# Three edits to a fused attention and feed-forward kernel: packed keys of later batches transposed by DMA, one first load of p, and k1's transposes between two sums

## The chip, the cores and the metric

The kernel runs on one NeuronCore of a Trainium2 chip. TensorE (PE) multiplies matrices and does transposes against an identity; its weight loads (PEld) overlap its matmuls. VectorE (DVE), ScalarE (ACT) and GpSimd (POOL) compute; SyncE (SP) issues DMAs, as POOL and ACT can. All DMAs of the core run on 16 DMA engines. The metric is the device time of one execution in microseconds (us), lower is better.

## The reference

The inputs are q, k and v of shape (8 batches, 8 heads, 576 rows, 64), p of shape (8, 8, 32, 64), and two weight matrices. Cut to what matters:

```python
def sm_attn(qq, kk, vv):                 # softmax attention, scale 1/8
    ...
p_packed = sm_attn(p, k, v)              # (8, 8, 32, 64): 32 packed keys per head
out = sm_attn(q, p_packed, p_packed)     # (8, 8, 576, 64)
x = out.transpose(0, 2, 1, 3).reshape(4608, 512)
h = x @ w_in                             # 512 -> 2048
result = (h * cos(h)) @ w_out            # 2048 -> 512
```

## The kernel before

All arithmetic on PE is in bf16 with f32 sums. A batch b passes through these steps, which the profile's lines name:

- `load` (L94) brings k, q and v into kbf, qbf and vbf, cast to bf16 on the way; POOL issues it. `pe_T` (L116) transposes k or q on PE, eight blocks to a group, three groups to a batch, and an engine copies each group into kT or qT (L85 on ACT, L87 on DVE). In later batches `xbar` (L102) does this with one DMA transpose, a crossing, issued on SP.
- `dup_p` (L386) casts p to bf16, `pack_p` (L131) transposes it into P2 (the tile P in the profile; DVE copies at L133).
- `s1` (L143, L152): scores of p against k and their exponential, with the row sums. `a1_pe` (L176) or `a1_xbar` (L166) transposes the result into a1T.
- `pp` (L186): the packed keys, 128 rows (four heads of 32) by two halves y of 64 columns, copied from PSUM into pp_sb as the column blocks y0, y1, y0. `pp_T` (L198) transposes the blocks (y0, y1) and (y1, y0) on PE, and DVE or ACT copies them into ppT.
- `s2` (L143, L231): scores of ppT against q and their exponential a2u. `sums2(b, y)` (L239, L241): one matmul pair with a block of ones gives the column sums of half y, and ACT takes their logarithm into lns. `normalise` (L247, L249): ACT's exponential of minus that, then DVE's product a2n.
- `ppw` (L213): PPW, the packed keys times w_in, in four column pieces n.
- `h_mm` (L263, L267, L270; `h_one`, L289 to L295, for batch 0): 16 chunks fc of h from PPW and a2n, the cosine on ACT, and DVE's product gT. `out_gen` (L351, L357): 16 matmuls of gT with w_out to an output chunk, a copy into osb, and the stores, issued on SP.

The order on every engine is written out by hand: each engine runs its instructions in program order. `warm(n)` (L391) puts n dummy matmuls on PE. The start (batch 0, then batch 1) runs from L393 to L488. From then on one batch's h is interleaved with the output matmuls of the batch before: `set_filler` queues the output matmuls of a batch, and `fill(n)` issues n of them. The loop body `slot(s, hooks, keep, heavy, last)` runs the 16 chunks of batch s; after chunk fc it issues its quota of output matmuls and calls the hooks of that step, and `last` is called between the last h matmuls and what follows them. Hook 7 is `tiled(s)`: two pieces of PPW, and `pp` of the next batch. Ahead of each slot s from 3 on stand `fill(5)`, `s2(s)`, `ppw`, `s1(s + 1)`, `a1_xbar(s + 1)`, `xbar("q", s + 1)`, `xbar("k", s + 2)` and `sums2`; POOL waits at `behind(...)` (L98) until the last crossing has landed and then issues the loads of the batches to come.

PSUM: the pool psA has three double banks, the pool O (the tile ot) two single banks; in the start `bank` hands out ot. The tiles pp_sb and ppT have two buffers each, by the parity of the batch.

Of the kernel before, what the change touches and what calls it, by code (L numbers as in the profile page):

```python
# [9 lines left out]
BF16 = mybir.dt.bfloat16  # L10
# [5 lines left out]
def kernel(  # L16
# [10 lines left out]
    nc = tc.nc  # L27
    B, H, S, D = q.shape
# [11 lines left out]
    const = ctx.enter_context(tc.tile_pool(name="const", bufs=1))  # L40
# [22 lines left out]
    V, ACT, G = nc.vector, nc.scalar, nc.gpsimd  # L63
# [3 lines left out]
    ident = const.tile([128, 128], BF16, name="ident")  # L67
# [3 lines left out]
    p_raw = const.tile([128, 2 * B, D], FP32, name="p_raw")  # L71
    p_bf = const.tile([128, 2 * B, 2, D], BF16, name="p_bf")
    a1 = [const.tile([128, 2, C, 128], BF16, name=f"a1_{i}") for i in range(2)]

    pp_sb = [const.tile([128, 3, D], BF16, name=f"pp_sb{i}") for i in range(2)]
    ppT = [const.tile([128, 2, H // 2, NP], BF16, name=f"ppT{i}") for i in range(2)]

    p_rows = p.rearrange("b h n d -> (b h n) d").rearrange("(g r) d -> r g d", r=128)
# [4 lines left out]
    def copy(eng, out, in_):  # L83
        if eng is ACT:
            ACT.copy(out=out, in_=in_)  # L85
        else:
            eng.tensor_copy(out=out, in_=in_)  # L87

    def psa(dt=FP32):
        return psum["A"].tile([128, 2, 512 if dt == FP32 else 1024], dt, name="psA", tag="A")  # L90

    def load(n, b):
        bf[n, b] = bf_pool.tile([TP, H, C * D], BF16, name=n + "bf", tag=n + "bf", bufs=1 if n == "q" else 2)
        G.dma_start(out=bf[n, b], in_=srcs[n][b].rearrange("h (p c) d -> p h (c d)", c=C))  # L94
# [12 lines left out]
    def pe_T(n, b, engs=(V, V, V), groups=(0, 1, 2), own=None):  # L107
        if 0 in groups:
            xT[n, b] = att_pool.tile([128, H * 3, TP], BF16, name=n + "T", tag=n + "T", bufs=2 if n == "k" else 1)
        t = xT[n, b]  # L110
        flat = bf[n, b].rearrange("p h x -> p (h x)")
        for i in groups:
            ps = own(BF16) if own else psa(BF16)[:, 0, :]
            for j in range(8):
                o = 8 * i + j
                nc.tensor.transpose(ps[:, j * TP:(j + 1) * TP], flat[:, o * 128:(o + 1) * 128],  # L116
                                    ident[0:TP, 0:TP])
            to = t[:, 8 * i:8 * i + 8].rearrange("p a x -> p (a x)"), ps[:, 0:8 * TP]
            if engs[i] is None:
                return to  # L120
            copy(engs[i], *to)

    def bank(dt=FP32):
        return O.tile([128, 512 if dt == FP32 else 1024], dt, name="ot", tag="ot")

    def pack_p(b0, b1, flat=None):
        ng = 2 * (b1 - b0)
        if flat is None:
            flat = psa(BF16).rearrange("p a x -> p (a x)")
        for g in range(ng):  # L130
            nc.tensor.transpose(flat[:, g * 128:(g + 1) * 128],  # L131
                                p_bf[:, 2 * b0 + g].rearrange("p t d -> p (t d)"), ident)
        V.tensor_copy(out=P2[:, b0:b1].rearrange("p b h n -> p (b h n)"), in_=flat[:, 0:ng * 128])  # L133
# [45 lines left out]
    def pp(b, eng=V, own=None):  # L179

        ps = own() if own else psa()[:, 0, :]
        for y in range(2):
            for j in range(C):
                c = 2 * (j % 3) + j // 3
                for x in range(4):
                    nc.tensor.matmul(ps[32 * x:32 * x + 32, y * D:(y + 1) * D],  # L186
                                     a1T[b][0:TP, y, j, 32 * x:32 * x + 32],
                                     bf["v", b][:, 2 * x + y, c * D:(c + 1) * D],
                                     start=(j == 0), stop=(j == C - 1))
        t = pp_sb[b % 2].rearrange("p a d -> p (a d)")  # L190
        copy(eng, t[:, 0:2 * D], ps[:, 0:2 * D])
        copy(eng, t[:, 2 * D:3 * D], ps[:, 0:D])

    def pp_T(b, eng=V, own=None):
        ps = own(BF16) if own else psa(BF16)[:, 0, :]
        t = pp_sb[b % 2].rearrange("p a d -> p (a d)")
        for i in range(2):
            nc.tensor.transpose(ps[:, i * 128:(i + 1) * 128], t[:, i * D:i * D + 128], ident)  # L198
        copy(eng, ppT[b % 2].rearrange("p i x n -> p (i x n)"), ps[:, 0:256])

    def ppw(b, n, eng=None, own=False, later=False, cuts=((0, 512),)):
# [25 lines left out]
    def s2(b):  # L227
        a2u[b] = att_pool.tile([128, 2, S], BF16, name="a2u", tag="a2u")
        ps = scores(lambda r, h, e: ppT[b % 2][r, (h + e) % 2, h // 2, :], xT["q", b])
        for y in range(2):  # L230
            ACT.activation(out=a2u[b][:, y].rearrange("p (e x) -> p e x", e=2),  # L231
                           in_=ps[y][:, :, 0:HS], func=AF.Exp, scale=rs1[b][:, y:y + 1])

    def sums2(b, y):
        if b not in lns:
            lns[b] = att_pool.tile([128, 2, S], FP32, name="lns", tag="lns")
        ps = psa()
        for e in range(2):
            nc.tensor.matmul(ps[:, e, 0:HS], ones_blk, a2u[b][:, y, e * HS:(e + 1) * HS],  # L239
                             start=True, stop=True)  # L240
        ACT.activation(out=lns[b][:, y].rearrange("p (e x) -> p e x", e=2),  # L241
                       in_=ps[:, :, 0:HS], func=AF.Ln)
# [141 lines left out]
    def dup_p(a, b, eng):  # L384
        for t in range(2):
            eng.tensor_copy(out=p_bf[:, a:b, t, :], in_=p_raw[:, a:b, :])  # L386

    def warm(n, wps=None, w=None):
        wps, w = bank() if wps is None else wps, wz if w is None else w
        for _ in range(n):  # L390
            nc.tensor.matmul(wps, w[:, 0:128], w, start=True, stop=True)  # L391

    nc.sync.dma_start(out=p_raw[:, 0:2, :], in_=p_rows[:, 0:2, :])  # L393
    load("k", 0)
    load("v", 0)
    make_identity(nc, ident)
    load("q", 0)
    G.dma_start(out=p_raw[:, 2:4, :], in_=p_rows[:, 2:4, :])
    load("k", 1)
    for n in range(3):  # L400
        load_w_in(n)
# [2 lines left out]
    wz4 = const.tile([128, 512], FP32, name="wz4")  # L404
# [6 lines left out]
        V.memset(t[:, :, :, TP:128], 0.0)  # L411

    warm(2, None, wz4)
    dup_p(0, 2, V)
    pack_p(0, 1)
    warm(1, None, wz4)
    warm(3)
    pe_T("k", 0, (V, ACT, V))
    s1(0)
    load_w_in(3)  # L420
    load("v", 1)
    warm(3)
    a1_pe(0)
    warm(2)
    recips(0)
# [1 line left out]
    warm(1)  # L427
    pp_T(0)
    pe_T("q", 0, (V, ACT, V))
    dup_p(2, 4, V)  # L430
    load("q", 1)
    for n in range(4):
        load_w_out(n)
    G.dma_start(out=p_raw[:, 4:, :], in_=p_rows[:, 4:, :])
    load("k", 2)
    s2(0)
    pack_p(1, 2, bank(BF16))
    warm(1)
    sums2(0, 0)
    sums2(0, 1)  # L440
    pe_T("k", 1, (V, V, V), own=bank)
    warm(1)
    normalise(0)
    s1(1)
# [45 lines left out]
    def slot(s, hooks, keep=0, heavy={}, last=None):  # L490


        left = to_do() - keep
        weight = [1 + heavy.get(fc, (0, 0))[0] for fc in range(NFC)]
        for fc in range(NFC):
            rest = h_mm(s, fc)
            if fc == NFC - 1 and last:
                last()
            rest()
            quota = (left * sum(weight[:fc + 1])) // sum(weight) - (left + keep - to_do())  # L500
            behind = min(quota, heavy[fc][1]) if fc in heavy else quota
            fill(quota - behind)
            while hooks and hooks[0][0] == fc:
                hooks.pop(0)[1]()
            fill(behind)
# [5 lines left out]
    def tiled(b):  # L511


        own, later = spare[0], []
        for n in (2, 3):
            later += ppw(b, n, (ACT, V)[n - 2], later=True)
        later[0]()
        pp(b + 1, V, own=lambda: own)
        later[1]()
# [10 lines left out]
    def cross(n, b):  # L530
# [41 lines left out]
                                in_=p_bf[:, 8:2 * B].rearrange("p g t d -> p (g t d)"))  # L572
# [7 lines left out]
    for s in range(3, B):  # L580
        nxt = s + 1 < B
        ACT.preload_act_table_set(EXP_SET)
        osb_eng[0] = V
        set_filler(s - 1)
        fill(5)
        s2(s)
        ppw(s, 0, V)
        fill(8 if nxt else 9)
        if nxt:
            s1(s + 1)  # L590
            ppw(s, 1, V)
            a1_xbar(s + 1)
            xbar("q", s + 1)
            recips(s + 1)
            if s + 2 < B:
                xbar("k", s + 2)
                behind(xT["k", s + 2][0:1, 0, 0:1])
        else:
            for n in range(1, 4):
                ppw(s, n, V)  # L600
        fill(4 if nxt else 5)
        sums2(s, 0)
        fill(5)
        sums2(s, 1)
        normalise(s)
        ACT.preload_act_table_set(SIN_SET)
        fill(13)
        osb_eng[0] = ACT
        for n, b in (("v", s + 2), ("q", s + 2), ("k", s + 3)):
            if b < B:  # L610
                load(n, b)
        if nxt:
            slot(s, [(7, lambda: tiled(s))], 5 if s % 2 else 13, {7: (5, 4)}, lambda: pp_T(s + 1, V))
        else:
            slot(s, [], 5)
    set_filler(B - 1)
# [32 lines left out]
```

## Time and profile before

| | |
|---|---|
| median of 3 runs | 245.64 us (244.95 to 245.83) |
| profiled execution | 245.78 us, its span 244.0 us, granted clock 1.0 |
| PE, DVE, ACT busy | 95%, 67%, 68% of the span |
| PE matmuls of L351, L263 | 485 of 379 ns, 448 of 286 ns (pipelined) |
| loads of k, q, v, median to landing | 13.6, 10.2, 7.8 us |
| crossings of qT, a1T, kT, median to landing | 6.1, 5.5, 4.9 us |

The profile is one execution. Times are counted from the start of its span. A matmul's duration is that of its whole way through the pipeline; matmuls follow each other sooner than that. Lines of the timeline give start, duration, engine, line, operation, output and input, how many instructions are merged, and in brackets the idle time of the engine before them and what ended it. In the DMA views q0 is the queue of POOL's DMAs, q1 that of SP's, and q8 brings instructions.

### The profile page before, as it was taken

To read this page: it belongs to the slowest core of one execution; us is meant where nothing else is said; L and a number is where in the kernel's file an instruction comes from. 1 tells how busy PE (TensorE), PEld (TensorE's weight loads), DVE (VectorE), ACT (ScalarE), POOL (GpSimd) and SP (SyncE) were. 2 spreads that over 40 slices of the span, in tenths; PEclk is the share of its full clock that TensorE was granted. 3 is DMA by queue.
4 is the path that set the end of the run, shared out by engine and by line. 5 is a ranking of instruction groups with operands and counts; after the bars stand their busy time and mean duration, and the time that the engine had idled before them with its cause. 6 is when DMAs were issued, how large, how long until landed. Compare 5 with 4: busy or idle time off the path is not lost.

```text
span 244.0 us, 5461 instructions
## 1 busy us (share of the span) xinstructions
PE 231.8 (95%) x2220; PEld 129.0 (53%) x2255; DVE 162.5 (67%) x259; ACT 166.0 (68%) x267; POOL 38.1 (16%) x61
## 2 busy tenths in 40 slices
PE   7978899999999999999999999999999999999994
PEld 3444254566446564556455654656455645665453
DVE  3349996777568786678758685878657878774001
ACT  2357999778568687877787697858797676774110
POOL 8523230210410032005100410030101010011000
PEclk9999999999999999999999999999999999999999
DMA  6999999999799999997999995999292111311133
GB/s 87 203 211 206 204 206 227 203 233 179 166 171 171 227 176 186 208 224 130 227 224 196 163 219 128 187 165 182 59 192 53 36 46 43 86 32 57 44 85 86
DMA packets 64152, 37.37 MB, mean 153 GB/s; under 512 B 36624, under 2 KB 59536, under 8 KB 64128
## 3 DMA queue, kind: packets, MB, share of 16 engines
q0 software_dynamic: 23184, 18.81, 50.6%
q1 hardware_dynamic: 40704, 18.09, 35.7%
q8 instruction: 17, 0.28, 0.5%
q10 hardware_dynamic: 240, 0.13, 0.2%
q14 instruction: 7, 0.06, 0.1%
HBM read 37.22 MB, written 9.44 MB: 191 GB/s over the span
## 4 chain that ended last, share of the span: by engine, by line
PE 81%; DVE 6%; issue 2%; ACT 1%; ACTq 0%
PE ot L351 48%; PE psA L263 22%; DVE gT L295 3%; PE psA L213 3%; PE psA L143 2%; PE psA L239 2%; PE ot L337 1%; PE psA L186 1%; DVE gT L270 1%; DVE PPW L87 1%; ACT cosT L267 1%; ACT cosT L294 0%; PE psA L116 0%; DVE qT L87 0%; PE psA L303 0%
## 5 line engine op out<-in xcount | busy, mean ns | idle before, releaser
L351 PE MATMUL ot<-w_out_bf,gT 128*128 128x512 bf16 x485 | 128.9, 379 | 2.2 <-issue 1.6
L270 DVE TENSOR_TENSOR gT<-psA,cosT 128x576 bf16<-128x576 f32 x112 | 83.3, 757 | 21.0 <-ACT cosT L267 19.9
L267 ACT ACTIVATE cosT<-psA 128x576 bf16<-128x576 f32 x112 | 72.9, 652 | 24.9 <-PE psA L263 23.5
L263 PE MATMUL psA<-a2n,PPW 128*128 128x288 bf16 x448 | 73.3, 286 | 0.3
L351 PEld LDWEIGHTS <-gT 128*128 128x128 bf16 x512 | 48.2, 98 | 39.5 <-issue 4.2
L263 PEld LDWEIGHTS <-PPW 128*128 128x128 bf16 x448 | 43.8, 98 | 30.1 <-issue 0.4
L87 DVE CAST PPW<-psA 128x1024 bf16<-128x1024 f32 (+1 forms) x24 | 26.8, 1132 | 6.8 <-PE psA L213 6.6
L85 ACT COPY osb<-ot 128x512 f32<-128x512 f32 (+1 forms) x23 | 13.1, 569 | 16.2 <-PE ot L351 13.2
L87 DVE COPY osb<-ot 128x512 f32<-128x512 f32 (+2 forms) x15 | 9.7, 645 | 20.3 <-PE ot L337 17.2
L274 POOL COPY joint<-gT 128x512 bf16<-128x512 bf16 x14 | 8.6, 616 | 83.8 <-DVE gT L270 83.8
L249 DVE SCALAR_TENSOR_TENSOR a2n<-a2u,r,lns 128x576 bf16<-128x576 bf16 x16 | 12.4, 815 | 9.2 <-ACT lns L247 9.2
L152 ACT ACTIVATE a<-psA 128x576 bf16<-128x576 f32 x16 | 10.2, 646 | 9.5 <-PE psA L143 9.5
L241 ACT ACTIVATE lns<-psA 128x576 f32<-128x576 f32 x16 | 10.3, 650 | 7.2 <-PE psA L239 6.7
L351 PE MATMUL ot<-w_out_bf,joint 128*128 128x512 bf16 x45 | 11.7, 380 | 0.2
L231 ACT ACTIVATE a2u<-psA,rs 128x576 bf16<-128x576 f32 x16 | 11.0, 736 | 1.1 <-PE psA L143 1.0
L98 POOL COPY gate<-kT 1x1 bf16<-1x1 bf16 x4 | 0.7, 178 | 68.0 <-DMA kT<-kbf 68.0
L247 ACT ACTIVATE lns<-lns 128x576 f32<-128x576 f32 x16 | 10.0, 673 | 0.0
L213 PE MATMUL psA<-w_in_bf,ppT 64*32 64x512 bf16 x224 | 9.8, 379 | 0.0
L391 PE MATMUL ot<-wz 128*128 128x512 bf16 (+1 forms) x15 | 8.0, 645 | 1.9 <-DVE wz L405 1.7
L295 DVE TENSOR_TENSOR gT<-psH,cosT 128x512 bf16<-128x512 f32 x15 | 9.3, 684 | 0.4 <-ACT cosT L294 0.4
L294 ACT ACTIVATE cosT<-psH 128x512 bf16<-128x512 f32 x15 | 8.4, 628 | 0.7 <-DVE gT L295 0.6
L289 PE MATMUL psH<-a2n,PPW 128*128 128x512 bf16 x28 | 7.3, 381 | 1.0 <-DVE PPW L87 0.8
(91 smaller groups left out, 171.9 us busy)
## 6 DMA issues: line engine op xcount, KB each, us to landing
kbf<-in_k_dram POOLq DMA_DIRECT2D x8, 576.0 KB, 13.6
vbf<-in_v_dram POOLq DMA_DIRECT2D x8, 576.0 KB, 7.8
qbf<-in_q_dram POOLq DMA_DIRECT2D x8, 576.0 KB, 10.2
out_dram<-osb SPq DMA_DIRECT2D x24, 192.0 KB, 2.8
out_dram<-osb SPq DMA_DIRECT2D x22, 128.0 KB, 2.4
w_in_bf<-in_moe_w_in_dram POOLq DMA_DIRECT2D x4, 512.0 KB, 16.7
w_out_bf<-in_moe_w_out_dram POOLq DMA_DIRECT2D x4, 512.0 KB, 20.7
out_dram<-osb SPq DMA_DIRECT2D x25, 64.0 KB, 2.2
```

Source lines behind the costliest of these rows:

```text
L85: ACT.copy(out=out, in_=in_)
L87: eng.tensor_copy(out=out, in_=in_)
L152: ACT.activation(out=a1[b % 2][:, y, :, 0:TP].rearrange("p (e m) x -> p e m x", e=2), in_=ps[y][:, :, 0:HS].rearrange("p e (m x) -> p e m ...
L213: nc.tensor.matmul(ps[y][32 * x:32 * x + 32, :], ppT[b % 2][r, 0, x, :], w_in_bf[r, x, n * 512:(n + 1) * 512], start=True, stop=True)
L231: ACT.activation(out=a2u[b][:, y].rearrange("p (e x) -> p e x", e=2), in_=ps[y][:, :, 0:HS], func=AF.Exp, scale=rs1[b][:, y:y + 1])
L241: ACT.activation(out=lns[b][:, y].rearrange("p (e x) -> p e x", e=2), in_=ps[:, :, 0:HS], func=AF.Ln)
L249: V.scalar_tensor_tensor(out=a2n[b][:, y], in0=a2u[b][:, y], scalar=r1[b][:, y:y + 1], in1=lns[b][:, y], op0=ALU.mult, op1=ALU.mult)
L263: nc.tensor.matmul(ps[:, e, 0:HS], PPW[b][:, y, fc * 128:(fc + 1) * 128], a2n[b][:, y, e * HS:(e + 1) * HS], start=(y == 0), stop=(y == 1))
L267: ACT.activation(out=csv, in_=ps[:, :, 0:HS], func=AF.Sin, bias=PI_HALF)
L270: V.tensor_tensor(out=gT[b][:, fc, :].rearrange("p (e x) -> p e x", e=2), in0=ps[:, :, 0:HS], in1=csv, op=ALU.mult)
L295: return lambda: V.tensor_tensor(out=gT[b][:, fc, 0:512], in0=ps, in1=cs, op=ALU.mult)
L351: nc.tensor.matmul(pss[c], w, w_out_bf[:, fc, :], start=(fc == 0), stop=(fc == NFC - 1))
```

## The change

Three edits, and what goes with them:

1. pp_sb has four column blocks, y0, y1, y1, y0. `pp` writes each half twice with one copy that reads its source twice; `pp_T` takes the blocks 0 to 1 and 2 to 3. For batches 4 to 7 (slots 3 to 6) `pp_T`, called at the end of the slot ahead, is dropped, and a hook at step 8 of that slot issues a crossing on SP from pp_sb to ppT. Batches 0 to 3 keep `pp_T`.
2. p of batches 0 and 1 comes in one first load on SP; POOL's second load, the second `dup_p` and the second `pack_p` go, and the first ones take both batches. Six dummy matmuls of the start go, and one of f32 with 192 columns comes in.
3. The first group of k1's transposes is issued on PE between `sums2(0, 0)` and `sums2(0, 1)`; the other two follow as before.

```diff
-    pp_sb = [const.tile([128, 3, D], BF16, name=f"pp_sb{i}") for i in range(2)]
+    pp_sb = [const.tile([128, 4, D], BF16, name=f"pp_sb{i}") for i in range(2)]
...
-        t = pp_sb[b % 2].rearrange("p a d -> p (a d)")
-        copy(eng, t[:, 0:2 * D], ps[:, 0:2 * D])
-        copy(eng, t[:, 2 * D:3 * D], ps[:, 0:D])
+        for y, to in ((0, pp_sb[b % 2][:, 0:4:3, :]), (1, pp_sb[b % 2][:, 1:3, :])):
+            copy(eng, to, ps[:, y * D:(y + 1) * D].unsqueeze(1).broadcast_to([128, 2, D]))
+
+    def pp_xbar(b):
+        nc.sync.dma_start_transpose(out=ppT[b % 2].rearrange("p i x n -> p i (x n)"),
+                                    in_=pp_sb[b % 2].rearrange("p a d -> p (a d)"))
...
-            nc.tensor.transpose(ps[:, i * 128:(i + 1) * 128], t[:, i * D:i * D + 128], ident)
+            nc.tensor.transpose(ps[:, i * 128:(i + 1) * 128], t[:, i * 128:(i + 1) * 128], ident)
...
-    def warm(n, wps=None, w=None):
+    def warm(n, wps=None, w=None, cols=512):
...
-            nc.tensor.matmul(wps, w[:, 0:128], w, start=True, stop=True)
+            nc.tensor.matmul(wps[:, 0:cols], w[:, 0:128], w[:, 0:cols], start=True, stop=True)
-    nc.sync.dma_start(out=p_raw[:, 0:2, :], in_=p_rows[:, 0:2, :])
+    nc.sync.dma_start(out=p_raw[:, 0:4, :], in_=p_rows[:, 0:4, :])
...
-    G.dma_start(out=p_raw[:, 2:4, :], in_=p_rows[:, 2:4, :])
...
-    dup_p(0, 2, V)
-    pack_p(0, 1)
+    dup_p(0, 4, V)
+    pack_p(0, 2)
     warm(1, None, wz4)
-    warm(3)
     pe_T("k", 0, (V, ACT, V))
...
-    warm(3)
+    warm(1, None, wz4, 192)
     a1_pe(0)
...
-    dup_p(2, 4, V)
...
     s2(0)
-    pack_p(1, 2, bank(BF16))
     warm(1)
     sums2(0, 0)
+    pe_T("k", 1, (V, V, V), (0,), own=bank)
     sums2(0, 1)
-    pe_T("k", 1, (V, V, V), own=bank)
+    pe_T("k", 1, (V, V, V), (1, 2), own=bank)
...
-            slot(s, [(7, lambda: tiled(s))], 5 if s % 2 else 13, {7: (5, 4)}, lambda: pp_T(s + 1, V))
+            slot(s, [(7, lambda: tiled(s)), (8, lambda: pp_xbar(s + 1))], 5 if s % 2 else 13, {7: (5, 4)})
```

## The prediction

> **What bounds the kernel now.** I read the page's engine table first, then busy time by stage, then the timeline of the start and of one slot's end, and last the DMA views.
>
> ```profile
> PE 231.8 (95%) x2220; PEld 129.0 (53%) x2255; DVE 162.5 (67%) x259; ACT 166.0 (68%) x267; POOL 38.1 (16%) x61
> PE 81%; DVE 6%; issue 2%; ACT 1%; ACTq 0%
> ```
> ```profile
> 0.00:36.00 36.00, 30.17 (x370) 15.25 (x377) 24.19 (x59) 22.57 (x43) 15.40 (x25) 1.00 1.17 186
> 98.00:124.00 26.00, 25.58 (x249) 14.42 (x252) 19.56 (x29) 19.90 (x32) 3.70 (x6) 1.00 1.13 203
> ```
>
> The second fence gives, after stage and length, PE, PEld, DVE, ACT and POOL busy, the clock, the DMA share and GB/s. From 98 to 124 us (slot 3 and what leads to it) PE is busy for 25.58 of 26.00 us: there a PE instruction less is time less, and a PE wait is time more. The first 36 us differ: PE has 5.8 us idle, part of the rest is dummy work (L391), and the DMA engines are full. The chain from 21.9 to 35.8 us runs almost wholly over DVE. So the start is priced by when DVE gets its data, the slots by PE.
>
> ```profile
> 5.00 0.79 POOL L94 DMA_DIRECT2D kbf<-in_k_dram  x1
> 17.10 0.41 PE L239 MATMUL psA<-a2u,ones_blk 128*128 128x288 bf16 x2 [0.23 <-ACT a2u L231]
> 17.97 0.85 PE L116 MATMUL ot<-ident,kbf 96*128 96x96 bf16 x16 [0.47 <-DMA kbf<-in_k_dram]
> 18.52 1.71 DVE L87 COPY kT<-ot 128x768 bf16<-128x768 bf16 x3 [2.04 <-PE ot L116]
> 20.14 1.54 DVE L249 SCALAR_TENSOR_TENSOR a2n<-a2u,r,lns 128x576 bf16<-128x576 bf16 x2
> ```
>
> PE waits for k1; DVE, idle for 2.04 us, then copies kT and only after it makes a2n, although ACT's exponentials (18.08 to 19.33) were ready. k1's landing at 17.9 sets the start.
>
> ```profile
> DMA to landing us min/median/max: 12.9/12.9/12.9
> ```
> ```profile
> q0 software_dynamic: 235, 0.24, 118.7%
> q8 instruction: 1, 0.02, 5.1%
> ```
>
> The first line is k1's load alone (5.00 + 12.9). Read in the same way, v0 lands at 10.4, q0 at 13.4, p's second part at 13.6. Equal loads are 2.9 to 3.0 apart, but k1 comes 4.3 after p: 1.3 too late. The other two lines are the queues from 15.8 to 17.0: a 16 KB instruction packet takes 5.1% of 16 engines x 1.2 us = 0.98 us of one engine, just where k1 ends. One late engine holds a whole load.
>
> **Start.** On SP p's first load doubles (64 to 128 KB). It landed at 2.64, the next copy of p is DVE's, and PE's dummies run to 5.30, so 0.4 us more is covered by 2.3. Two more L131 transposes (0.11 each) take the place of dummies, with PE waiting for k0 until 7.6 anyway: nothing. Batch 0's pp copies: the second grows from 0.21 to 0.29, and the first transpose now needs both, up to 0.2 later; but q0's transposes, which set the next step, start at 13.5 when q0 lands, so 0.05 to 0.1 remains, inside ACT's wait. The dup and pack of batch 1 leave DVE (0.61 + 0.29) and PE at 15.2 to 16.5, where ACT's exponential was late anyway: nothing.
>
> On POOL's queue p's second part no longer stands ahead of k1: 13.6 - 13.4 = 0.2 us less. The larger question is the instruction packet. There are 17 in all for about 4,500 PE instructions, so they follow PE's count, and 7 to 11 PE instructions fewer stand before this one. The packet comes no earlier, k1's last bytes 0.2 earlier. Bounds: it still hits (k1 at 17.7) or misses (13.6 - 0.2 + 3.0 = 16.4). Since it touched only the last of 16 engines and the two move apart, I take 16.4.
>
> Then k1's first eight transposes (0.42, half of the 0.85 row) run after the first sum, at 16.75; the second sum starts at 17.2 for 17.1, while ACT is in the first Ln until 17.55: covered. DVE copies kT from 17.4; the third group waits for a bank until the first copy ends, so the copies end at 19.1 and a2n (1.54) at 20.6, for 21.7: 1.0 us. DVE carries this to 33, where q1 stops it: its load (14.99 + 18.3 = 33.3, now 33.1) was used at 33.92. **Start: -0.75 us**, as PE's first w_out matmuls (w_out1 lands at 38.8, ninth matmul at 39.4) still fit. If k1 is hit, the second sum, queued on PE behind k1, comes at 18.2; ACT and DVE then end as before: -0.05.
>
> **Slots 3 to 6.**
>
> ```profile
> 115.78 0.65 PE L263 MATMUL psA<-a2n,PPW 128*128 128x288 bf16 x4
> 116.33 0.27 PE L198 MATMUL psA<-ident,pp_sb 128*128 128x128 bf16 x2
> 116.44 1.67 PE L351 MATMUL ot<-w_out_bf,gT 128*128 128x512 bf16 x6
> 118.05 0.14 PEld L143 LDWEIGHTS <-ppT 64*32 64x32 bf16 x16 [0.42 <-DVE gT L270]
> ```
>
> h's last four start 0.12 apart, so PE is free at 116.27; the next real work starts at 116.44. The two transposes cost 0.17 here; in slots 4 to 6 they start without that wait, 0.11. Sum: **-0.5 us** (0.44 to 0.68). DVE loses the ppT copy (0.28) and gains 0.08 in pp_sb, both beside ACT's work: nothing. s2 of the next batch (L143) must then find ppT by 118.05 - 0.75 - 0.15 = 117.15.
>
> The crossing goes on SP. Queued behind it are output stores (L357) alone, with four output buffers, so a late store costs nothing. What is queued ahead counts:
>
> ```profile
> 105.49 3.07 SPq L102 DMA_TRANSPOSE kT<-kbf  x1
> 108.65 11.01 SPq L357 DMA_DIRECT2D out_dram<-osb  x8
> ```
> ```profile
> L357 SPq DMA_DIRECT2D out_dram<-osb x1: 2127/2127/2127, 109.8 to 109.8; - x1
> DMA to landing us min/median/max: 5.6/5.6/5.6
> ```
> ```profile
> P<-p_bf SPq DMA_TRANSPOSE x1, 4.0
> ```
>
> Four stores stand ahead after kT's issue. Three take 0.4 to 0.6 us, but the third took 2.13 (next-to-last fence), while another instruction packet stood in the engines. The crossing issues at 110.9 if that is not repeated, at 112.5 if it is; pp_sb is ready by 109.7. POOL's next loads are issued from 111.1. No trace row has a crossing of two blocks. Nearest below is a 64 KB store (2.2), nearest above without loads the eight-block crossing (4.0); beside loads, stores issued at 111.9 and 112.6 landed 6.3 later, and the twelve-block a1T took 9.1 at 96.3 and 12.1 at 69.7. I take 110.9 + 4.0 = 114.9, 2.2 us to spare, because PE's lower count moves that packet too. Slot 4: issue near 135, stores there took 5.3 to 6.3, so 141.3; needed at 144.56 - 1.0 = 143.5. Slot 5: 162.4 + 5.0 = 167.4; needed 170. Slot 6 has no loads.
>
> The Trainium skill (DMA: Bandwidth & Descriptors, Queues, rings and completion order) says that an engine alternates between queues after a packet of some 9 to 17 descriptors, at most 64. The queue row above makes one load descriptor 1.187 x 16 x 1.2 / 235 = 0.097 us, so by the page's usual 17 a crossing would lose an estimated 1.6 us to loads, 112.5 + 4.0 + 1.6 = 118.1; by its ceiling 6.2. The measured 6.3 of the stores lies between, and my sums use only that.
>
> **Sum.** 245.78 (profiled execution; span 244.0 and 1.78 around it) - 0.75 - 0.5 = 244.5; the median of the runs is 0.14 lower, 245.64, so **244.4** as a median. 0.5% is 1.23 us, about what a measurement of this kernel can tell from no change: the forecast stands right at that edge, own range 243.7 to 245.0 (a start gain of 1.0 if q1 doesn't stop it, less if it does sooner).
>
> **Rivals.**
> - k1 is still hit by the packet: -0.05 - 0.5, 245.1. For it: the packet was there in this profile; against: both shifts lead away from it.
> - The crossing is issued behind the held store, beside the loads: 112.5 + 6.3 = 118.8, PE waits 1.65 at L143 in slot 3: -1.25 + 1.65, 246.0. For it: SP was held in the profile. Against: nothing but the moved packet.
> - Slower: a crossing beside loads takes as long as a1T's, 9.1. From 112.5 it lands at 121.6, a wait of 4.45, and 245.64 - 1.25 + 4.45 = 248.8; from 110.9 a wait of 2.85, 247.2. It decides from a landing after 119.6, where the wait passes 1.25 + 1.23. Slots 4 and 5 then move with slot 3 and add little. Against it: a1T has six times the blocks.
>
> **How the numbers follow.** Forecast 0.52 (of it 0.40 faster by over 0.5%, the rest within), k1 hit 0.14 (within), held crossing 0.18 (0.14 within, 0.04 slower), long crossing 0.16 (slower). Faster 0.40, within 0.40, slower 0.20. The range runs from 243.5, below the forecast's own, to 246.9, which takes in two rivals and leaves out most of the third.
>
> **What would show it.** Right: L116 on kbf at about 16.8 before the second L239, DVE's kT copy near 17.4, L351 from 35.8; no L198 after slot 2; L143 starting within 0.15 us of L351's end in all slots. Wrong: L116 again at 17.7 or later; a PE gap before L143 near 117 ended by the DMA of ppT; ppT landing over 6 us after issue; or an L351 held by w_out.

## The result, and the profile after

The kernel after runs at a median of 247.44 us (11 executions, 245.75 to 252.62) against 245.53 for the kernel before (11, 244.95 to 245.90); the ratio is 1.0074, 95% interval 1.0053 to 1.0095. That is slower by over 0.5%, and outside the range given. The ratio leaves out the three executions that lie over 1.5% above the fastest, all of them among the half-clock executions described below, so it understates the loss. The profiled execution took 248.57 us, with a span of 246.8.

The page of the kernel after, first its busy line, then the shares of the chain by engine and the granted clock in 40 slices:

```profile
PE 234.9 (95%) x2243; PEld 128.7 (52%) x2243; DVE 161.9 (66%) x252; ACT 166.1 (67%) x267; POOL 37.5 (15%) x60
PE 78%; DVE 6%; DMA 4%; ACT 1%; issue 1%; ACTq 0%
PEclk9999999999999999999999988999999999999998
```

PE is counted busy for 3.1 us longer than before although it was given fewer instructions (x2243 stands against x2220 because before's profile lacks some records, such as 27 of the 512 of L351, so the two sums are not strictly alike). A DMA has 4% of a chain that had none, and the clock dips around slices 24 and 25, at 142 to 154 us. By stage (stage, length, PE, PEld, DVE, ACT and POOL busy, clock, DMA share, GB/s):

```profile
0.00:36.00 36.00, 30.17 (x388) 15.36 (x389) 24.39 (x56) 23.29 (x44) 15.19 (x25) 1.00 1.18 186
98.00:124.00 26.00, 26.00 (x252) 14.37 (x251) 19.45 (x28) 20.07 (x33) 3.71 (x6) 1.00 1.10 194
124.00:151.00 27.00, 24.98 (x238) 13.26 (x237) 17.53 (x24) 18.10 (x29) 3.72 (x6) 0.94 1.13 179
```

Only the stage with slot 4 (124 to 151) has lost something: 2.02 us of PE idle, and a mean clock of 0.94. The chain of work names the step, and PE's timeline the wait behind it:

```profile
134.46 0.97 PE ot L354 x4
135.43 0.49 PE psA L266 x4
135.92 0.08 PE ot L354
136.00 9.65 DMA ppT<-pp_sb
145.65 0.04 issue
145.69 0.44 PE psA L143 x16
```
```profile
142.64 1.03 PE L354 MATMUL ot<-w_out_bf,joint 128*128 128x512 bf16 x4
145.69 0.44 PE L143 MATMUL psA<-qT,ppT 64*32 64x288 bf16 x16 [2.02 <-DMA ppT<-pp_sb]
```

The crossing of batch 5 was issued at 136.00 and landed 9.65 us later. PE had finished its last output matmul at 143.67 and waited for ppT until 145.69. The next lines cut the time along three stretches of 3.41 us, in the same columns as above:

```profile
143.04:146.45 3.41, 1.39 (x28) 0.46 (x27) 0.74 (x2) 1.58 (x2) 0.62 (x1) 1.00 1.15 157
146.45:149.86 3.41, 3.41 (x16) 1.06 (x22) 1.28 (x2) 1.00 (x2) 0.00 (x0) 0.50 1.09 198
149.86:153.27 3.41, 3.41 (x40) 1.66 (x25) 2.07 (x4) 2.33 (x6) 0.00 (x0) 1.00 0.38 85
```

After the wait the clock stood at half speed for one stretch of 3.41 us: PE counts as busy throughout, but gets half as much done. So the wait of 2.02 us is paid for nearly twice, with 1.80 more at half clock (table below).

The lead of after over before, from the starts of the same exponential (a2u of s2) or logarithm (lns) on ACT, gives the whole balance of the two profiled executions:

| place | after minus before, us | this step |
|---|---|---|
| s2 of batch 1 (36 us) | -0.67 | start |
| sums2 of batch 3 and s2 of batch 4 (97 to 118) | -0.68 | nothing |
| sums2 of batch 4 (122) | -0.85 | two transposes gone, -0.17 |
| s2 of batch 5 (146) | +0.96 | the wait, 2.02 less what slot 4 saves |
| sums2 of batch 5 (152) | +2.76 | half clock, +1.80 |
| sums2 of batch 7 (205) | +2.53 | two slots at -0.11 and -0.12 |
| last copy of DVE (243) | +2.53 | nothing |
| end | +2.78 | +0.25, with only stores left |

245.78 + 2.78 = 248.56, against 248.57 measured.

### The profile page after: what moved, and what is told of

It is laid out like the page before. It is cut to its first block, busy times and chain, and to the rows that moved or that the text cites. A ratio compares the mean times of both kernels' runs of the same rounds, so it can differ in the third digit from the quotient of the medians.

```text
span 246.8 us, 5473 instructions
## 1 busy us (share of the span) xinstructions
PE 234.9 (95%) x2243; PEld 128.7 (52%) x2243; DVE 161.9 (66%) x252; ACT 166.1 (67%) x267; POOL 37.5 (15%) x60
## 4 chain that ended last, share of the span: by engine, by line
PE 78%; DVE 6%; DMA 4%; ACT 1%; issue 1%; ACTq 0%
PE ot L354 48%; PE psA L266 20%; DMA ppT<-pp_sb 4%; DVE gT L298 3%; PE psA L216 3%; PE psA L143 2%; PE psA L242 1%; PE ot L340 1%; PE psA L186 1%; DVE gT L273 1%; DVE PPW L87 1%; ACT cosT L270 1%; ACT cosT L297 0%; PE psA L116 0%; DVE qT L87 0%
## 5 line engine op out<-in xcount | busy, mean ns | idle before, releaser
L354 PE MATMUL ot<-w_out_bf,gT 128*128 128x512 bf16 x512 | 134.0, 379 | 0.0
L266 PE MATMUL psA<-a2n,PPW 128*128 128x288 bf16 x448 | 73.3, 286 | 0.0
L354 PEld LDWEIGHTS <-gT 128*128 128x128 bf16 x512 | 48.3, 98 | 39.6 <-issue 4.2
L266 PEld LDWEIGHTS <-PPW 128*128 128x128 bf16 x448 | 43.8, 98 | 30.1 <-issue 0.4
L354 PE MATMUL ot<-w_out_bf,joint 128*128 128x512 bf16 x48 | 13.7, 418 | 0.0
L234 ACT ACTIVATE a2u<-psA,rs 128x576 bf16<-128x576 f32 x16 | 11.0, 736 | 3.0 <-PE psA L143 2.8
L216 PE MATMUL psA<-w_in_bf,ppT 64*32 64x512 bf16 x224 | 9.8, 379 | 0.0
L394 PE MATMUL ot<-wz 128*128 128x512 f32 (+2 forms) x13 | 7.6, 669 | 1.9 <-DVE wz L407 1.7
L292 PE MATMUL psH<-a2n,PPW 128*128 128x512 bf16 x30 | 7.8, 381 | 0.8 <-DVE PPW L87 0.8
```

What stands on the lines that cost most here:

```text
L216: nc.tensor.matmul(ps[y][32 * x:32 * x + 32, :], ppT[b % 2][r, 0, x, :], w_in_bf[r, x, n * 512:(n + 1) * 512], start=True, stop=True)
L266: nc.tensor.matmul(ps[:, e, 0:HS], PPW[b][:, y, fc * 128:(fc + 1) * 128], a2n[b][:, y, e * HS:(e + 1) * HS], start=(y == 0), stop=(y == 1))
L354: nc.tensor.matmul(pss[c], w, w_out_bf[:, fc, :], start=(fc == 0), stop=(fc == NFC - 1))
```

## The experiments

Each kernel was timed against the kernel before on the same chip. Lines behind `pp` carry numbers higher by 3 or more than in the kernel before: L216 is ppw's matmul, L354 the output matmul, L266 h's, L234 the exponential of s2.

**Which edit loses.** First the kernel after without edit 1's crossing (batches 4 to 7 again through `pp_T`):

```diff
-slot(s, [(7, lambda: tiled(s)), (8, lambda: pp_xbar(s + 1))], 5 if s % 2 else 13, {7: (5, 4)})
+slot(s, [(7, lambda: tiled(s))], 5 if s % 2 else 13, {7: (5, 4)}, lambda: pp_T(s + 1, V))
```

> The changed kernel with pp_T put back for batches 4 to 7: only the start's edits (one first load of p, k1's transposes between the sums) and the four-block pp_sb are left. Theory (the crossing alone loses the time, by landing behind POOL's loads in slots 3 to 5): the start's lead of 0.67 us is kept to the end, so about 244.9 against 245.5, no wait at L143 over 0.2 us and the granted clock at 1.0 throughout. Rival (the start's edits lose by themselves, k0 landing 0.55 later, and the profiled lead was one lucky execution): 245.5 or more.

Measured: 245.24 us, ratio 0.9994 (0.9984 to 1.0004); before stood at 245.33 in this series. No wait for ppT over 0.2 us is left on PE. Then edit 1 alone, with the start as it was before:

> The kernel before with the first edit alone: crossings for batches 4 to 7, the old start. Theory: the crossings land at the same times (their place is set by the loads), but PE arrives 0.7 us later, so the wait in slot 4 is some 1.3 us for 2.0 and the clock falls in fewer executions: 246 to 247.5, with a spread of over 2 us between executions. Rival (the loss comes from the two parts together, the crossing by itself is harmless): 245.0, 0.5 faster than before.

Measured: 248.79 us, ratio 1.0110 (1.0074 to 1.0146), with a wait of 2.04 us in slot 4, and not the 1.3 expected: with the old start PE came to that place no later (its wait began at 143.64 us, for 143.67). The crossing makes the whole loss. The two edits of the start, -0.67 in the trace, show as 0.1 in the medians, within the interval; more on that below.

**Is it the loads around the crossing?** The loads of slots 3 to 5 are held on POOL until the crossing has landed:

```diff
+def loads():
+    if s + 2 < B:
+        behind(ppT[(s + 1) % 2][0:1, 0, 0, 0:1])
+    for n, b in (("v", s + 2), ("q", s + 2), ("k", s + 3)): ...
-slot(s, [(7, lambda: tiled(s)), (8, lambda: pp_xbar(s + 1))], ...
+slot(s, [(7, lambda: tiled(s)), (8, lambda: pp_xbar(s + 1)), (8, loads)], ...
```

> The changed kernel with POOL's loads of slots 3 to 5 issued after the crossing of that slot has landed (a gate on ppT, after the hook of step 8) and not ahead of the slot. Theory (a crossing is late only because loads stand ahead of it in the DMA engines): each crossing lands 2.5 to 4.5 us after its issue, no wait at L143, clock 1.0, 244.3 to 244.7. Rival (a crossing of two blocks is slow there whatever else runs): landings of 7 us or more again and over 246. Second rival (the loads, 3 to 4 us later, are then late themselves): no wait for ppT, but waits for kT, qT or a1T, 245 to 247.

Measured: 244.95 us (12 executions, of which eleven at 244.68 to 245.49 and one at 247.24), ratio 0.9994 (0.9978 to 1.0010). That is 0.25 above the range expected (244.3 to 244.7), but the loss is gone, and the same six stores still stand ahead of the crossing. Slot 4 in the trace, POOL's timeline, with the kernel after first:

```profile
134.89 0.77 POOL L94 DMA_DIRECT2D vbf<-in_v_dram  x1 [0.36 <-PE psA L186]
135.77 0.77 POOL L94 DMA_DIRECT2D qbf<-in_q_dram  x1
136.53 0.77 POOL L94 DMA_DIRECT2D kbf<-in_k_dram  x1
```
```profile
140.52 0.18 POOL L98 COPY gate<-ppT 1x1 bf16<-1x1 bf16 x1 [3.96 <-DMA ppT<-pp_sb]
141.07 0.77 POOL L94 DMA_DIRECT2D vbf<-in_v_dram  x1 [0.37 <-PE psA L266]
```

And the DMA view, of the first 5.0 us of the crossing in the kernel after, and of the whole crossing (138.0 to 140.5) with the loads behind:

```profile
DMA packets 918, 0.85 MB, mean 170 GB/s; under 512 B 56, under 2 KB 775, under 8 KB 917
```
```profile
DMA packets 429, 0.29 MB, mean 115 GB/s; under 512 B 321, under 2 KB 321, under 8 KB 429
ppT<-pp_sb SPq DMA_TRANSPOSE x1, 2.3
```

Alone, the crossing is some 320 packets under 512 bytes, landed in 2.3 us. Beside loads issued 1.1 us ahead of it, at most 56 such packets moved in its first 5 us; the rest followed from 141 us on, as v's load neared its end (144.5). Over all kernels, twelve crossings of slots 3 to 5 with the loads behind landed in 2.3 to 3.4 us; of eleven with the loads not held, ten took 4.4 to 9.65. The four of slot 3 among the eleven show how the order of issue counts: 0.83 us ahead of the first load the crossing took 2.4 us, 0.60 and 0.59 ahead 4.4 each, and 0.01 ahead 8.0.

The Trainium skill (DMA: Bandwidth & Descriptors, Queues, rings and completion order) was weighed in the prediction. Its usual packet length had put a crossing's delay at an estimated 1.6 us, its ceiling at 6.2; the runs show 9.65 - 2.32 = 7.3, beyond both.

Next, the crossing in slot 6 alone, where no load follows:

> The changed kernel with the crossing in slot 6 alone (batch 7, no loads beside it), and pp_T for batches 4 to 6. Theory: that crossing lands about 3.5 us after its issue with 5 us to spare, PE loses two transposes (0.11 us), so 0.1 below the kernel without crossings, about 244.8. Rival (a crossing costs by itself, through SP or the stores behind it): above the kernel without crossings by 0.3 us or more.

Measured: 244.96 us, ratio 0.9993 (0.9983 to 1.0002), landing after 3.4 us with no wait. And the loads held in slot 4 alone:

> The kernel after with the loads held behind the landing of the crossing in slot 4 alone; in slots 3 and 5 they stay ahead. If the crossing of slot 4 makes the whole loss: landing at about 140.5 there, no TensorE wait, and the time of the kernel with all loads behind, 244.95; the crossings of slots 3 and 5 land in 4 to 8 us, as late as 120.1 and 172.6, without a wait. If the loss only moves to the next crossing beside loads: the one of slot 5, wanted at about 170, lands later than that, with a wait of 1 us and more, and 246 or above.

Measured: 245.23 us (12 executions, 244.82 to 248.60), ratio 0.9994 (0.9979 to 1.0008). The large loss was slot 4's, but part of it moved on. Slot 4's crossing now landed in 2.3 us. Slot 5's took 6.8, landing at 171.0 for 170.2:

```profile
PE psA L143 <- DMA ppT<-pp_sb: 0.8, 1, 0.8
```

In the kernel after, where it took 7.4, slot 4's own delay had hidden that one.

**What a wait costs by itself.** Without any crossing, ppT of batch 5 was made late by copies on GpSimd (one, two or three dummies):

```diff
+def last(b):
+    pp_T(b, V)
+    if b == 5:
+        G.tensor_copy(out=hold[:, 0:256], in_=flat)           # flat: ppT of batch 5
+        for _ in range(1):                                    # or 2, or 3
+            G.tensor_copy(out=hold[:, 512:1024], in_=hold[:, 0:512])
+        G.tensor_copy(out=flat, in_=hold[:, 0:256])
```

> The kernel without the crossing (ppT back on TensorE and VectorE), and in slot 4 alone ppT of batch 5 then goes through three copies on GpSimd (out, a dummy of 128x512, back), so that it is ready late without any transfer. The copy on VectorE ended at 143.07 us and TensorE wanted ppT at 143.8; a copy of 128x512 on GpSimd took 0.62. Estimate: ready at 144.6, a TensorE wait of 0.8. If a wait costs only its length: 245.24 + 0.8 = 246.0. If the clock falls after any wait, 1.8 more in the executions where it does: up to 247.8.

> The same late ppT in slot 4 with two dummy copies: between the one that made TensorE wait 0.67 us (no execution of 11 at a mean clock below 0.994) and the one that made it wait 2.01 us (2 of 6 below). Estimate: a wait of 1.35. If the half clock comes with any wait above about 1 us: median 246.7, and some executions at 248.2 with a mean clock of 0.993. If it needs a wait near 2 us: 246.7 in all, none below 0.994.

> The same with three dummy copies instead of one: ready at about 145.8, a TensorE wait of 2.0, as long as the one behind the crossing, but with no crossing in the kernel. If the half clock belongs to the wait: 245.24 + 2.0 = 247.2 in executions at full clock and 249.0 where a stretch of 3.4 us at half clock follows, in a third of them or more. If it belongs to the crossing or to the DMA traffic: 247.2 in all, with a mean clock of 0.998 and above.

| dummies | wait of PE, us | median, us | ratio | executions with a mean clock below 0.994 |
|---|---|---|---|---|
| 1 | 0.67 | 245.99 | 1.0023 (1.0013 to 1.0034) | 0 of 11 |
| 2 | 1.34 | 246.64 | 1.0051 (1.0037 to 1.0064) | 0 of 5 |
| 3 | 2.01 | 247.52 | 1.0106 (1.0079 to 1.0133) | 2 of 6 (248.83, 249.03) |

Two executions with three dummies and no crossing lost as much clock as the kernel after, while no execution of before in any series fell below 0.997: the half clock belongs to the wait and needs no crossing. It comes in some executions only. In the profiled one with three dummies, the wait of 2.01 us left the clock alone:

```profile
142.04:145.45 3.41, 2.01 (x13) 0.88 (x10) 1.73 (x4) 2.47 (x4) 2.03 (x4) 1.00 1.21 173
145.45:148.87 3.42, 2.81 (x56) 1.21 (x56) 1.51 (x2) 1.38 (x3) 1.11 (x3) 1.00 1.25 232
```

These cuts are not chosen freely. In the traces' records of the granted clock every stretch at full clock is a whole multiple of 3.413 us (after: 139.95 = 41 of them; before: 238.93 = 70), so the clock is decided on a fixed grid whose place against the kernel differs from one execution to the next. Here the wait was cut in two by the grid, 1.40 and 0.61, and PE was busy for 2.01 us or more of each window. In the kernel after (above), and in the one with the crossing alone, the whole wait fell into one window with 1.39 and 1.37 us busy, and the next window ran at half. With two dummies the whole wait of 1.34 fell into one window too, which left 2.07 us busy, and the next ran at full clock. The crossing alone first, then two dummies:

```profile
142.43:145.84 3.41, 1.37 (x22) 0.53 (x28) 1.01 (x2) 1.78 (x2) 0.61 (x1) 1.00 1.37 183
145.84:149.25 3.41, 3.41 (x31) 1.09 (x16) 1.22 (x1) 1.37 (x2) 0.00 (x0) 0.50 1.22 227
```
```profile
144.10:147.51 3.41, 2.07 (x32) 0.95 (x32) 1.23 (x1) 1.86 (x3) 1.79 (x4) 1.00 1.25 220
147.51:150.92 3.41, 3.41 (x40) 1.56 (x39) 2.08 (x4) 2.02 (x5) 0.00 (x0) 1.00 0.46 96
```

So the same wait of 2.0 us costs 2.0 us or 3.8, by where it falls: 4 of 6 executions of the crossing alone and 5 of 11 of the kernel after have a mean clock of 0.993 or less. The spread of the kernel after follows this: six executions with a mean clock of 0.997 and above at 245.75 to 247.44 us, five at 0.993 and below at 248.57 to 252.62. Single executions of three kernels with loads held behind a crossing fell as low (0.983, 0.986 and 0.991, one of 11 or 12 each), and so did two of eight of the one with k4's load held too (0.993, below). None of these has a trace, so what wait they had is not known.

**Two attempts to keep the crossing and lose the wait.** In the first, eight output matmuls of the filler go ahead of s2:

```diff
-        fill(5)
+        fill(13)
         s2(s)
         ppw(s, 0, V)
-        fill(8 if nxt else 9)
+        fill(0 if nxt else 1)
```

> The kernel after, with eight output matmuls of the slot before (8 x 0.216 = 1.7 us) moved from behind s2 and the first ppw group to ahead of s2 in slots 3 to 7, so that ppT is wanted 1.7 us later; the loads stay ahead of the crossing. If only the wait in slot 4 makes the loss: it shrinks from 2.0 to 0.3, the half clock goes, and the time is that of the kernel without the crossing plus 0.3 less 0.5: about 245.0. If ScalarE's exponentials, then 1.7 later, become the next bound: 246 to 248 with waits on ScalarE and none on ppT.

Measured: 251.65 us, ratio 1.0257 (1.0239 to 1.0275). No wait on ppT is left, although slot 4's crossing again took 7.9 us; but there is now nothing between s2 and s1 to cover ScalarE's exponentials, and PE waits for them in each slot, 5.1 us in all by the trace. The time is above the 246 to 248 expected; the rest of the 6.2 us by which PE ends later than without the crossing is not accounted for. The largest part of the waits:

```profile
PE psA L143 <- ACT a2u L234: 3.4, 8, 0.5
```

In the second, the kernel with the loads behind also has k4's load in slot 2 held behind a1T of batch 3:

```diff
     load("q", 3)
-    load("k", 4)
...
     a1_xbar(3)
+    behind(a1T[3][0:1, 0, 0, 0:1])
+    load("k", 4)
```

> The kernel whose loads of slots 3 to 5 come behind the crossing, and in slot 2 the load of k4 moved behind the landing of a1T of batch 3, which in every kernel so far was issued at 69 us among three loads, landed with the last of them (81.3 to 82.8) and was wanted at 81.6 to 82. If the landing of a crossing on SP's queue is set by the loads around it: a1T lands by about 78 us, no TensorE wait at 82, and the lead over before that the three crossings bring (0.5 us) is kept: 244.5 to 244.7, with fewer executions above 245. If not: 244.95 as the kernel that it is made from, or slower where k4 then lands late (its crossing was issued at 82).

Measured: 247.04 us, ratio 1.0076 (1.0049 to 1.0104). The first half of the theory held: a1T landed at 78.4 instead of 80.7 to 82.8, and slot 2 had no wait. But k4 landed at 87.0 instead of 81, its crossing at 92.0 instead of 88, and slot 3's loads, gated on that, were issued at 93.2 instead of 89. a1T of batch 4 went out at 97.9, among them, and took 12.1 us:

```profile
PE psA L186 <- DMA a1T<-a: 1.9, 1, 1.9
```

A load that is held back shifts the next gate, and the next crossing meets the loads.

**The start by itself.** The kernel with the loads behind, with the old start, and with edit 3 alone:

> The kernel before with the crossing and the loads behind it, and nothing of the two edits of the start. The first traces gave the start edits 0.67 us, but the kernel with the crossing alone reached s2 of batch 1 at 35.95 us with the old start too, as early as the others. If the start edits bring nothing beyond the executions in which the packet of the instructions hits k1: 244.9 to 245.2, as 244.95 with them. If they bring what was forecast: 245.6.

> The same with k1's first transposes between the sums but p still in two loads. In the four kernels with one load of p, k0 landed at 8.0 to 8.1 us instead of 7.5, and batch 0 began 0.55 later. If k1's position matters by itself: up to 0.3 us below the same kernel with the old start, 244.7. If s2 of batch 1 is set by q1's landing (32.7 to 33.4) in all of them: the same time within 0.2.

Measured: 245.26 us (ratio 0.9998, 0.9990 to 1.0007) and 244.96 (0.9993, 0.9978 to 1.0008), beside 244.95 with both edits, from the earlier series. s2 of batch 1 began at 35.95 and 36.14 us in the two profiles with the crossing and the old start, at 36.03 with edit 3 alone, and at 35.89 to 36.17 in the ten with both edits. Before's profile, 36.66, is the odd one: of fourteen profiled executions it is the only one in which k1 landed at 17.9; in all others it was 16.3 to 17.1. The prediction took an instruction packet for the cause. But such a packet runs at this place in all fourteen profiles: it starts at 15.8 to 16.6 us, in thirteen of them before k1 has landed, and takes 0.95 to 0.97 us. Here it is, from 15.8 to 17.0, in the kernel with the crossing alone, the same line as the prediction showed for before, while k1 landed at 16.32:

```profile
q8 instruction: 1, 0.02, 5.1%
```

So the packet's being there is not enough to make k1 late, and what held k1 in before's execution is not shown. What the edits do when k1 isn't late is seen where the chain of the start turns to DVE's first PPW copies, in the kernel after and in the one with the crossing alone:

```profile
21.16 1.13 DVE PPW L87 x3
```
```profile
21.13 1.12 DVE PPW L87 x3
```

The two come at the same time: nothing is gained. With one load of p, k0 landed at 8.13 and k1 at 16.87; with two, at 7.46 and 16.32. Batch 0's first exponential came 0.67 us later with one load (10.35 for 9.68), and from the first sum to a2n the kernel after took 2.40 us (17.02 to 19.42) for 3.05 (16.34 to 19.39). What k1's transposes gain between the sums, 0.65, the late start of batch 0 takes. The profile with edit 3 alone can't show more: there k0 had landed at 7.56, but its transposes came behind PE's dummies at 8.23, and batch 0 was as late (10.40). Whether edit 3 alone is worth the 0.3 between the two medians stays open, as the intervals overlap.

The best of these, 244.95 and 244.96, lie 0.4 to 0.5 below before's median, but no interval excludes 1. The forecast's gain on the transposes, 0.5, is there in the traces and too small for these times to tell from no change; that of the start is not there.

## Why the prediction was wrong

- **The two transposes: right.** -0.17 in slot 3 and -0.11 and -0.12 in slots 5 and 6, as forecast; slot 4 shows -0.12 where the loads come behind.
- **The start: right against the trace by luck, and not as a gain.** k1 landed at 16.87 (forecast 16.4) and the step gave -0.67 (forecast -0.75). But k1's late landing was a mishap of before's profiled execution: with the old start and the crossing alone k1 came at 16.32 and s2 of batch 1 at -0.71, with an instruction packet at the same place. A delay seen in one execution was counted as if every execution had it, and put down to a packet that all of them have.
- **p's doubled load: costed at nothing, and it isn't free.** k0 landed at 7.96 to 8.31 us in the ten profiles with one load of p, at 7.46 to 7.66 in the four with two. That takes back what edit 3 gains. (Edit 2 was tested as a whole; the size of the load was not varied by itself.)
- **Slot 3: in time, with some luck.** The crossing went out at 111.7 (forecast 110.9), 0.60 us ahead of the first load, and landed at 116.1 (forecast 114.9); the third store was held again, for 1.44. In the kernel of the first attempt above, crossing and first load went out together (111.43 and 111.44), and it took 8.0.
- **Slot 4: the step that failed.** "Slot 4: issue near 135, stores there took 5.3 to 6.3, so 141.3; needed at 144.56 - 1.0 = 143.5." The issue was at 136.0, the need at 143.67, and the landing at 145.65: the term of up to 6.3 us, taken from stores, was 9.65 for a crossing beside the loads. A crossing lands as the loads let it. The row that said so was in the trace of before and was quoted in the prediction: a1T, 12.1 us from 69.7, landed at 81.8 with k's load at 81.3. It was set aside because a1T has six times the blocks, but size is not what these times hang on: two blocks took 2.3 to 9.65 us, by what ran beside them.
- **Slot 5: the same term, wrong too.** 5.0 us was taken and 7.4 measured (issued at 165.2, landed at 172.6). With slot 4 mended, PE waited 0.8 us there. The prediction says that its sums use only the stores' 6.3, but they took 4.0 in slot 3 and 5.0 here.
- **The slower rival** had the mechanism and the price (9.1), but put it in slot 3, where the crossing is issued ahead of the loads, and said of the others "Slots 4 and 5 then move with slot 3 and add little". They were in more danger: in slot 4 the loads go out 1.1 us before the crossing, in slot 5 2.2.
- **A wait's price** was its length in every sum of the prediction. Here 2.0 us cost 3.8 when it fell into one window of the clock. Nothing in before's trace showed that, since PE had no wait of that size after 36 us.

## What to carry to other kernels

Ask of a transfer on a latency path not how large it is but what is queued on the same DMA engines when it is issued, or within the next microsecond; the best row to price it from is the one with the same neighbours, not the one with the same size. On a PE-bound kernel a wait of 0.67 or 1.34 us cost its length, and one of 2 us its length plus, in some executions, half of a 3.4 us stretch. A gain that comes from one late landing in one profile has to be seen in the spread of the times before it is counted.

## What the runs showed of the hardware

- The clock of PE is set in windows of 3.413 us that do not start with the kernel. A window in which PE was busy for 1.37 or 1.39 us was followed by one at half clock; windows with 2.01 and 2.07 us were not. The windows in which PE's work ends narrow it: 1.56 us busy (crossing alone, from 241.41) and 1.69 (before, from 238.75) were followed by full clock, 0.95 (after, from 242.02) by half. Where between 1.39 and 1.56 the limit lies is open. An estimate from these: with PE busy otherwise, a wait below 3.41 - 1.56 = 1.85 us does not bring the half clock. The Trainium skill (TensorE: Matmul & The Clock Gate, What's actually happening) gives a free-running window of 3413 ns, which the traces confirm, and names an idle window of about 3.4 us as the condition for half speed; the runs show that PE need not be idle for the whole of it.
- A crossing of 64 KB landed in 2.3 to 3.7 us with no load under way and in 9.65 among three loads of 576 KB, two issued ahead of it and one 0.5 us after. Issued 0.6 us ahead of the loads it still took 4.4, and level with the first of them 8.0.
- An instruction packet of 16 KB took one DMA engine for 0.95 to 0.97 us from 15.8 to 16.6 us on in all fourteen profiles. Why k1 landed at 17.9 beside it in one of them, and at 16.3 to 16.5 in the three others with two loads of p, stays open.
